# Freeing space for the down weights, x first and one weight order for all tiles in a fused attention + gated-layer kernel

## The chip, the cores and the metric

The kernel runs on one core of a Trainium2 chip. The metric is device time in microseconds (us); lower is better. Every run quoted is fast, that is, within 1.5% of the fastest run of the same kernel. PE is TensorE, ACT is ScalarE, DVE is VectorE, SP is the queue that issues most transfers.

## The reference, cut to what matters

```python
# S = 2048 tokens, D = 1024; H = 32 query heads of Dh = 32, ONE key/value head; F = 3584; bf16
def A(x):   # attention on the normalised x
    q = x @ wq; k = x @ wk; v = x @ wv
    p = softmax(einsum("bhqd,bkd->bhqk", q, k) * Dh**-0.5)
    return einsum("bhqk,bkd->bhqd", p, v) @ wo
def B(x):   # gated layer on the normalised h
    return (sigmoid(x @ w_gate) * (x @ w_up)) @ w_down
h  = x + A(layernorm(x))
h2 = h + B(layernorm(h))
```

There are 16 tiles of 128 tokens. A tile's scores go in 32 *visits*: one visit is 8 PE matmuls (scores) and two ACT exponentials of 128x1024. In all there are 512 visits and 1024 exponentials.

## The kernel before

The order of every instruction is fixed when the program is built. The kernel contains a small planner: it keeps a clock for each engine, adds an assumed cost for each instruction, and emits on PE whatever its clocks say is ready. Score matmuls have priority, so that ACT never runs dry; the gated layer (gate/up "GU", down "D") fills the rest, and when the planner thinks that nothing is ready it emits a *filler* matmul. The main loop, cut:

```python
while True:
    t = pl.free["pe"]
    ...
    if can_s and run - t < 750.0:      # ACT's queue is short: emit the scores of visit v
        emit_S(v); v += 1; emit_PV(t); continue
    ...                                # else go on with the current group, or pick one:
    # PRIO = ["xT", "KV", "Q0", "OP", "GU", "D", "Q"]
    ...
    if v and spare:                    # nothing is ready: filler
        pl.op("pe", mm(F_ps[:, spare[0], 0:256], ident[:, :], kT4[:, 0:256], True, True), ...)
```

One memory zone is used twice: first for the normalised, transposed x (four quarters), wq and the K/V weights, later for all 28 pieces of w_down:

```python
wq_sb = zview(DT * S, DT, D)
...
def free_wd(last):                      # called as projections finish
    for i in list(wd_left):             # 7 groups of 4 pieces
        if (i < 4 and q_left4[i] == 0 and 2 * i in k_ev and 2 * i + 1 in k_ev) or \
                (i >= 4 and q_left[0] == 0 and len(k_ev) == NT // 2):
            wd_left.remove(i); load_wd(4 * i, 4, [last])
```

Gate/up weights go through a ring of 22 pieces of 256 KB. A piece is kept while the planner sees a use ahead that is near. The order of uses was special for the first two tiles, so that they share pieces; D of any tile needs all of w_down:

```python
TP = [(0, p) for p in range(5)] + [(1, 4), (1, 3), (0, 5), (1, 5), (0, 6), (1, 6)] + [(1, p) for p in (2, 1, 0)]
TP += [(t, p) for t in range(2, NT) for p in (reversed(range(NFP)) if t % 2 else range(NFP))]
```

The softmax row sums of the first four groups (a group is eight of the 32 heads for one tile) were made on PE, by matmuls with a matrix of ones (cut). Later groups add on DVE and use four such matmuls. The start:

```python
load_x([0]); load_x([1])
wk_ld = dma(lambda: ACT.dma_start(wk_sb, ...), "wk", ..., ring="act")
wv_ld = dma(lambda: ACT.dma_start(wv_sb, ...), "wv", ..., ring="act")
load_wq(0, 2); load_x([2, 3]); load_wq(2, 4); load_x([4, 5])
...
if v == 0 and known([c_id, c_w], t):   # warm-up matmuls until the first transposes are ready
    pl.op("pe", mm(S_ps[:, 5, :], ident[:, :], hact[:, 0:512], True, True), [c_id, c_w], **t_mm(512))
```

The softmax here doesn't subtract the row's maximum and nothing guards it: scores larger than these inputs give would overflow.

Of the kernel before, what the change touches and what calls it, by code (L numbers as in the profile page):

```python
# [128 lines left out]
def bass_sequential_preLN__grouped_kv_mqa__glu_gated_glu__prompt_kernel(  # L129
# [21 lines left out]
    NI = 2 * NFP  # L151
    TP = [(0, p) for p in range(5)] + [(1, 4), (1, 3), (0, 5), (1, 5), (0, 6), (1, 6)] + [(1, p) for p in (2, 1, 0)]
    TP += [(t, p) for t in range(2, NT) for p in (reversed(range(NFP)) if t % 2 else range(NFP))]
    ITEMS = [(t, p, w) for t, p in TP for w in range(2)]
# [6 lines left out]
    NPS = 16  # L161
    NX = 4
    NB = 3
    NPC = 22
# [8 lines left out]
    with ExitStack() as es:  # L173
# [43 lines left out]
        def xnT(dt, a, n):  # L217
            return xnT4[a // 512][:, dt, a % 512:a % 512 + n]
        wq_sb = zview(DT * S, DT, D)
        o3 = DT * S + DT * D  # L220
# [73 lines left out]
        def load_wq(a, b, deps=()):  # L294
            o = dma(lambda: SP.dma_start(wq_sb[:, :, a * P:b * P], A_wq[:, a * P:b * P].rearrange("(a p) n -> p a n", p=P)),
                    f"wq{a}", D * P * (b - a) * 2, deps, prio=0)
            for g in range(a, b):
                wq_ld[g] = o

        load_x([0])  # L300
        load_x([1])
        wk_ld = dma(lambda: ACT.dma_start(wk_sb, A_wk.rearrange("(a p) j -> p a j", p=P)), "wk", P * DT * DH * 6, prio=0,
                    ring="act")
        wv_ld = dma(lambda: ACT.dma_start(wv_sb, A_wv.rearrange("(a p) j -> p a j", p=P)), "wv", P * DT * DH * 6, prio=0,
                    ring="act")
        load_wq(0, 2)
# [76 lines left out]
        def mm(o, l, r, start, stop, **kw):  # L383
            return lambda: PE.matmul(o, lhsT=l, rhs=r, start=start, stop=stop, **kw)  # L384

# [45 lines left out]
        q_left4 = [2 * NG, 2 * NG, NG, NG]  # L431
        wd_ld = []

        def mk_KV(p):
# [27 lines left out]
        def mk_Q(g, tok, n):  # L462
            def atoms(b):
                return [(mm(F_ps[:, b, 0:n], wq_sb[:, dt, g * P:(g + 1) * P], xnT(dt, tok, n),
                            dt == 0, dt == DT - 1), n, []) for dt in range(DT)]

            def after(b, last):
                q_left[0] -= 1
                q_left4[tok // 512] -= 1
                free_wd(last)  # L470
                early_loads(last)
                if tok == 0:
                    fa, fd = both(QTb[:, :, g, :], F_ps[:, b, 0:256].rearrange("p (a b) -> p a b", a=2))
                    ev = evac(fa, fd, 256, [last], 1)
                    q_ready[0][g] = q_ready[1][g] = ev
                else:
                    k = len(q_store)
                    s = k % NQS
                    deps = [last] + ([q_store[k - NQS]] if k >= NQS else [])
                    fa, fd = both(qst[:, s, 0:n], F_ps[:, b, 0:n])  # L480
                    ev = evac(fa, fd, n, deps, 1)
                    q_store.append(dma(lambda: SP.dma_start(q_dram[:, g, tok:tok + n], qst[:, s, 0:n]),
                                       f"qs{s}", P * 2 * n, [ev], prio=2))
                    for t in range(tok // P, (tok + n) // P):
                        q_of[t].append(q_store[-1])
                        load_q(t)
                return [ev]
            first = lambda: [wq_ld[g]] + [xT_ev[k] for k in range(tok // P, (tok + n) // P)]
            return Group("Q0" if tok == 0 else "Q", atoms, first, after)
# [20 lines left out]
        def free_wd(last):  # L510
            for i in list(wd_left):
                if (i < 4 and q_left4[i] == 0 and 2 * i in k_ev and 2 * i + 1 in k_ev) or \
                        (i >= 4 and q_left[0] == 0 and len(k_ev) == NT // 2):
                    wd_left.remove(i)
                    load_wd(4 * i, 4, [last])
# [39 lines left out]
        def reclaim(v):  # L555
            for sl, own in list(slot_owner.items()):
                if own in pv_done and (own[0] < NX or slot_add.get(sl) is not None):
                    slot_rel[sl] = [pv_done[own], slot_add.get(sl)]
                    del slot_owner[sl]
                    p_free.append(sl)  # L560
            if visits[v][0] >= NX:
                for sl in [sl for sl in p_free if sl >= NPS]:
                    p_free.remove(sl)

        def emit_S(v):
            G, kq = visits[v]
            qb, g = G // ND, 2 * (G % ND)
            deps = s_ready(v)
            pl.free["pe"] += 95.0
            last = None  # L570
            for kk in range(KB):
                for j in range(4):
# [5 lines left out]
                                 deps if (kk == 0 and j == 0) else [], occ=27.4, lat=27.4 + 150.0 + SEM)  # L578
            pl.free["pe"] += 111.0
            for i in range(2):  # L580
# [21 lines left out]
        sum_ev = {}  # L602
        sum_todo = collections.deque((G, kq) for G in range(NX, NT * ND) for kq in range(1, VPG))

        def flush_sums():
            while sum_todo:
                G, kq = sum_todo[0]
                if n_exp_of[G] <= kq or (kq == 1 and G > NX + 1 and (G - 2, 1) not in pv_done):
                    return
                sum_todo.popleft()  # L610
                for i in range(2):
                    T = Ts[:, G % 2, i * 1024:(i + 1) * 1024]
                    ins = [kq - 1, kq] if kq == 1 else [kq]
                    src = [pslot(slot_of[(G, q, i)]) for q in ins]
                    deps = [exp_of[(G, q, i)] for q in ins]
                    deps.append((pv_done.get((G - 2, 1)) if G > NX + 1 else None) if kq == 1 else sum_ev[(G, kq - 1, i)])
                    a, b = (src[0], src[1]) if kq == 1 else (T, src[0])
                    o = pl.op("dve", lambda T=T, a=a, b=b: DVE.tensor_tensor(out=T, in0=a, in1=b, op=ALU.add), deps,  # L618
                              prio=4, **t_dve(1024, 1.92))
                    for q in ins:  # L620
                        slot_add[slot_of[(G, q, i)]] = o
                    sum_ev[(G, kq, i)] = o
# [10 lines left out]
        def mk_PV(G, h):  # L633
            qb, g = G // ND, 2 * (G % ND)

            def block(b):
                r, rs = [], []
                k0, k1 = 8 * h, 8 * h + 8
                for kt in range(k0, k1):
                    kq, kk = kt // KB, kt % KB  # L640
                    for j in range(4):
# [3 lines left out]
                                    kt == k0, kt == k1 - 1, tile_position=(0, DH * j)))  # L645
                        if G < NX:
                            rs.append(mm(F_ps[DH * j:DH * (j + 1), b, 256:512], ones[:, :], pslot(slot)[:, co:co + 256],
                                         kt == k0, kt == k1 - 1, tile_position=(0, DH * j)))
                for j in range(4 if G >= NX and h else 0):
                    r.append(mm(F_ps[DH * j:DH * (j + 1), b, 256:512], ones[:, :],  # L650
                                Ts[:, G % 2, j * 512:j * 512 + 256], True, True, tile_position=(0, DH * j)))
# [46 lines left out]
            def first():  # L698
                r = [exp_of[(G, kq, i)] for kq in range(VPH * h, VPH * (h + 1)) for i in range(2)]
                r += [v_ev.get(p) for p in range(4 * h, 4 * h + 4)]  # L700
                return r + [c_v1] + ([merge_ev.get(G)] if G >= NX and h else [])

# [4 lines left out]
        def emit_PV(t):  # L707
# [8 lines left out]
            b = min(banks, key=lambda b: max([0.0] + [o.end for o in bank_rel[b]]))  # L716
            deps = gr.first() + list(bank_rel[b])
            for fn in gr.atoms(b):
                o = pl.op("pe", fn, deps, occ=27.4, lat=27.4 + 220.0 + SEM)
                o.tag = "PV"  # L720
                deps = []
            pl.free["pe"] += 109.0
            bank_rel[b] = gr.after(b, o)
# [42 lines left out]
        def flush_hT():  # L766
            while late_hT and (late_hT[0] < 2 or (late_hT[0] - 2) in gu_last):
# [4 lines left out]
                for i in range(len(ITEMS)):  # L772
                    if ITEMS[i][0] == t if t > 1 else (ITEMS[i][0] < 2 and t == 0):
                        queues["GU"].append(mk_GU(i))
# [146 lines left out]
        while True:  # L921
# [15 lines left out]
            if sd is None and queues["PV"]:  # L937
                pl.free["pe"] += 95.0
                if emit_PV(t):
                    idle = 0  # L940
                    continue
                pl.free["pe"] -= 95.0
            if cur is not None:
                fn, n, deps, *cb = cur[1][cur_i]
                if known(deps, t) or not can_s:
                    o = pl.op("pe", fn, deps + (cur[2] if cur_i == 0 else []), **t_mm(n))
                    o.tag = cur[0].cls
# [33 lines left out]
            if v == 0 and known([c_id, c_w], t):  # L981
                pl.op("pe", mm(S_ps[:, 5, :], ident[:, :], hact[:, 0:512], True, True), [c_id, c_w], **t_mm(512))
                continue
            idle += 1
            spare = [b for b in range(2) if known(bank_rel[b], t) and (cur is None or b != cur_b)]
            if v and spare:
                pl.op("pe", mm(F_ps[:, spare[0], 0:256], ident[:, :], kT4[:, 0:256], True, True), [k_ev[0]] + list(bank_rel[spare[0]]), **t_mm(256))
                continue
# [108 lines left out]
```

## Time and profile before

The time was 1109.71 us (1109.67 to 1110.74 in three runs).

| what | before |
|---|---|
| first exponential | 19.8 us |
| last projection matmul of Q ends, gated layer starts | 136 us |
| visit 480 of 512 starts | 964.8 us |
| last exponential ends | 1028 us |
| end of the profiled run | 1109.1 us |

Visits are found by counting blocks of eight score matmuls in the timeline of PE. Caution: in this trace 166 of the 12306 PE matmul records are missing (12140 matmuls stand beside 12306 weight loads), so PE's busy time is too small by a little; the transfers, ACT and the score matmuls are complete.

The table of stretches of before: start and end, length, then busy us (and instructions) of PE, weight loads, DVE, ACT and POOL, then PE's granted clock, share of DMA and GB/s. The first row is from the middle, the second from the tail.

```profile
400.00:440.00 40.00, 38.70 (x480) 16.93 (x486) 34.96 (x68) 39.98 (x45) 1.15 (x2) 1.00 0.75 185
...
1040.00:1080.00 40.00, 38.72 (x177) 17.51 (x180) 9.27 (x18) 4.18 (x7) 0.79 (x2) 1.00 1.10 267
```

In the middle ACT has no idle time and PE hardly any. In the tail ACT's exponentials are done and PE works off the gated layer. The same view for two stretches that the change touches:

```profile
58.00:92.00 34.00, 32.95 (x636) 21.92 (x634) 14.51 (x36) 33.24 (x37) 0.00 (x0) 1.00 0.81 247
150.00:180.00 30.00, 27.57 (x348) 12.85 (x350) 26.46 (x53) 29.26 (x33) 1.33 (x2) 1.00 1.00 252
```

The start, from the timeline of before (start, length, engine, line, operation, out<-in, count, and in brackets the idle time ahead of it with what ended it):

```profile
0.72 0.46 ACTq L302 DMA_DIRECT2D zone<-in_A_wk_dram  x1
...
1.67 10.94 PE L384 MATMUL S_ps<-hact,ident 128*128 128x512 bf16 x40 [1.67 <-POOL ident L278]
...
4.32 1.33 ACT L315 ACTIVATE zone<-zone 128x256 bf16<-128x256 bf16 x4 [0.98 <-DMA zone<-in_A_wk_dram]
...
8.57 0.88 DVE L371 TENSOR_SCALAR ring<-ring,rstd 128x1024 bf16<-128x1024 bf16 x2
...
12.44 1.06 PE L389 MATMUL F_ps<-ident,ring 128*128 128x128 bf16 x16
...
19.37 0.40 PE L384 MATMUL S_ps<-QTb,kT 32*128 32x256 bf16 x8
...
19.82 1.94 ACT L588 ACTIVATE Pr<-S_ps 128x1024 bf16<-128x1024 f32 x2 [0.73 <-PE S_ps L384]
```

x is normalised at 9.45 us (8.57 + 0.88), but its transposes stand behind 40 warm-up matmuls until 12.4. wk had arrived at 4.3.

What happens when Q is done, first on the SP queue, then on PE (two timelines of before):

```profile
144.29 2.94 SPq L493 DMA_DIRECT2D zone<-in_B_w_down_dram  x6
...
151.17 0.82 SPq L493 DMA_DIRECT2D zone<-in_B_w_down_dram  x2
152.04 2.74 SPq L817 DMA_DIRECT2D ring<-in_B_w_up_dram  x2
```

```profile
151.75 2.03 PE L384 MATMUL F_ps<-kT,ident 128*128 128x256 bf16 x17
...
157.74 0.39 PE L384 MATMUL F_ps<-ring,hnT 128*128 128x512 bf16 x1 [1.14 <-DMA ring<-in_B_w_up_dram]
```

The ring gets its first refill only after the last down weights. PE runs out of weights: 17 fillers in a row, then a wait.

The chain of waits, in its last stretch (start, length, what):

```profile
1030.35 4.84 DMA ring<-in_B_w_gate_dram
1035.24 9.89 PE F_ps L384 x45
...
1074.52 5.10 DMA ring<-in_B_w_gate_dram
1079.66 9.89 PE F_ps L384 x45
```

The end is PE's, with two waits for ring pieces in it.

### The profile page before, as it was taken

The numbers are of one execution on the slowest core, as the hardware profiler recorded it, in microseconds if no ns is written. First come the engines' busy times: TensorE is split into PE (matmuls) and PEld (weight loads), VectorE is DVE, ScalarE is ACT, GpSimd is POOL, SyncE is SP. The second block draws the span as 40 slices with busy tenths as digits, with TensorE's granted clock in tenths as the row PEclk, the third lists the DMA queues.
The fourth block names the chain that finished last, engine by engine and source line by source line (L and its number), as shares of the span: only waits on it lengthen the run. The fifth ranks groups of instructions, "written<-read, shape, count | busy, mean of one in ns | idle before, by whom it ended". The sixth has DMA issues, their size and how long they took to land.

```text
span 1109.1 us, 29973 instructions
## 1 busy us (share of the span) xinstructions
PE 1061.8 (96%) x12140; PEld 475.8 (43%) x12306; DVE 884.5 (80%) x1727; ACT 1011.6 (91%) x1162; POOL 27.9 (3%) x56
## 2 busy tenths in 40 slices
PE   9999989999999999999999999999999999999998
PEld 5664344343344444444444444444444444344443
DVE  7747988798888989798888989798888988788411
ACT  4999999999999999999999999999999999999110
POOL 1100000000000000000000000000000000000000
PEclk9999999999999999999999999999999999999999
DMA  9976399928769595968869595977869595976991
GB/s 231 202 236 199 99 255 282 275 53 232 206 144 251 144 253 131 262 189 196 238 149 247 142 257 130 259 194 188 242 149 243 149 251 138 253 190 180 260 264 43
DMA packets 304730, 222.06 MB, mean 200 GB/s; under 512 B 121552, under 2 KB 295888, under 8 KB 304592
## 3 DMA queue, kind: packets, MB, share of 16 engines
q1 hardware_dynamic: 302512, 220.01, 78.4%
q8 instruction: 97, 1.59, 0.6%
q10 hardware_dynamic: 2080, 0.13, 0.1%
q14 instruction: 41, 0.34, 0.1%
HBM read 189.66 MB, written 7.86 MB: 178 GB/s over the span
## 4 chain that ended last, share of the span: by engine, by line
PE 82%; ACT 8%; issue 4%; DVE 4%; DMA 2%; SPq 0%; POOL 0%; POOLq 0%
PE F_ps L384 68%; PE S_ps L384 14%; ACT Pr L588 8%; DMA ring<-in_B_w_gate_dram 1%; ACT tnh L860 1%; DVE Ts L618 1%; DMA ring<-in_B_w_up_dram 1%; DVE st L325 1%; DVE st L323 0%; DVE ring L371 0%; DVE ring L364 0%; DVE hact L274 0%; SPq L817 0%; DVE hst L864 0%; DVE mv L327 0%
## 5 line engine op out<-in xcount | busy, mean ns | idle before, releaser
L588 ACT ACTIVATE Pr<-S_ps 128x1024 bf16<-128x1024 f32 x1014 | 951.4, 1054 | 6.6 <-PE S_ps L384 5.6
L618 DVE TENSOR_TENSOR Ts<-Ts,Pr 128x1024 bf16<-128x1024 bf16 x720 | 475.3, 679 | 40.6 <-ACT Pr L588 36.9
L384 PE MATMUL F_ps<-ring,hnT 128*128 128x512 bf16 x1671 | 418.4, 381 | 19.3 <-issue 11.7
L384 PEld LDWEIGHTS F_ps<-ring,hnT 128*128 128x128 bf16 x1754 | 149.7, 98 | 223.0 <-issue 79.1
L384 PE MATMUL F_ps<-zone,hact 128*128 128x512 bf16 x839 | 210.2, 381 | 6.3 <-issue 6.0
L384 PE MATMUL S_ps<-QTb,kT 32*128 32x256 bf16 x4096 | 203.4, 273 | 8.9 <-ACT Pr L588 5.6
L384 PEld LDWEIGHTS S_ps<-QTb,kT 32*128 32x128 bf16 x4096 | 61.0, 92 | 192.1 <-ACT Pr L588 131.9
L384 PE MATMUL F_ps<-Pr,Vb 128*32 128x256 bf16 x4056 | 134.5, 274 | 0.1
L864 DVE SCALAR_TENSOR_TENSOR hst<-tnh,F_ps 128x512 bf16<-128x512 f32 x112 | 76.5, 683 | 62.9 <-PE F_ps L384 60.1
L384 PEld LDWEIGHTS F_ps<-zone,hact 128*128 128x128 bf16 x896 | 76.2, 98 | 103.7 <-issue 32.3
L860 ACT ACTIVATE tnh<-F_ps 128x512 f32<-128x512 f32 x112 | 71.3, 637 | 46.6 <-PE F_ps L384 46.6
L384 PEld LDWEIGHTS F_ps<-Pr,Vb 128*32 128x32 bf16 x4056 | 97.1, 96 | 36.4 <-DVE hst L864 10.9
L618 DVE TENSOR_TENSOR Ts<-Pr 128x1024 bf16<-128x1024 bf16 x120 | 80.5, 688 | 37.3 <-ACT Pr L588 37.1
L384 PE MATMUL F_ps<-zone 128*128 128x256 bf16 (+2 forms) x568 | 74.2, 274 | 5.1 <-DVE mvr L335 1.2
L384 PE MATMUL F_ps<-wo_sb,OT 128*128 128x512 bf16 x239 | 59.6, 380 | 2.5 <-issue 2.5
L384 PEld LDWEIGHTS F_ps<-zone 128*128 128x128 bf16 x576 | 42.6, 97 | 29.5 <-issue 8.8
L894 DVE SCALAR_TENSOR_TENSOR h_sb<-F_ps,h_sb 128x512 bf16<-128x512 f32 x32 | 21.9, 685 | 35.6 <-PE F_ps L384 35.6
L625 DVE TENSOR_TENSOR Ts<-Ts 128x1024 bf16<-128x1024 bf16 x60 | 41.4, 689 | 1.5
L337 POOL TENSOR_SCALAR zb<-mvb 128x1 bf16<-128x1 bf16 (+1 forms) x24 | 10.5, 437 | 1012.5 <-DVE mvb L333 1012.5
L384 PEld LDWEIGHTS F_ps<-wo_sb,OT 128*128 128x128 bf16 x256 | 22.4, 98 | 29.3 <-issue 6.7
L685 DVE STREAM_TRANSPOSE Rc<-Ri 128x256 f32<-128x256 f32 x64 | 28.1, 439 | 0.1
L668 DVE TENSOR_TENSOR Oc<-F_ps,Oc 128x256 f32<-128x256 f32 x60 | 25.2, 420 | 3.5 <-PE F_ps L384 2.1
(59 smaller groups left out, 349.0 us busy)
## 6 DMA issues: line engine op xcount, KB each, us to landing
ring<-in_B_w_gate_dram SPq DMA_DIRECT2D x308, 256.0 KB, 4.0
ring<-in_B_w_up_dram SPq DMA_DIRECT2D x307, 256.0 KB, 4.3
zone<-in_B_w_down_dram SPq DMA_DIRECT2D x28, 256.0 KB, 3.9
h_sb<-in_A_x_dram SPq DMA_DIRECT2D x16, 256.0 KB, 5.3
out_dram<-h_sb SPq DMA_DIRECT2D x32, 128.0 KB, 2.6
ring<-in_A_x_dram SPq DMA_DIRECT2D x7, 512.0 KB, 5.6
QTb<-q_scratch SPq DMA_DIRECT2D x14, 256.0 KB, 4.5
Pr<-in_B_w_up_dram SPq DMA_DIRECT2D x9, 256.0 KB, 4.0
```

Of the source, the lines that this page charges most:

```text
L325: b = pl.op("dve", lambda k=k, src=src: DVE.bn_stats(st[:, k, 1, :], src[:, 512:1024]), dep, prio=prio, occ=590, lat=756, order=[st_user.g ...
L337: f = pl.op("pool", lambda: POOL.tensor_scalar(out=zb[:, ph, sl].unsqueeze(2), in0=mvb[:, ph, sl, 1:2], scalar1=LN_EPS_BF16, scalar2=None, ...
L384: return lambda: PE.matmul(o, lhsT=l, rhs=r, start=start, stop=stop, **kw)
L588: exps[u] = pl.op("act", lambda slot=slot, pb=pb: ACT.activation(out=pslot(slot).rearrange("p (a b) -> p a b", a=2), in_=S_ps[:, pb:pb + 2 ...
L618: o = pl.op("dve", lambda T=T, a=a, b=b: DVE.tensor_tensor(out=T, in0=a, in1=b, op=ALU.add), deps, prio=4, **t_dve(1024, 1.92))
L625: merge_ev[G] = pl.op("dve", lambda T4=T4: DVE.tensor_tensor(out=T4[:, :, 0, :], in0=T4[:, :, 0, :], in1=T4[:, :, 1, :], op=ALU.add), [sum ...
L668: a = pl.op("dve", lambda: DVE.tensor_tensor(out=Oc[:, :], in0=O, in1=Ob, op=ALU.add), [last, oc_ev[G], o_ev.get(G - 1)], prio=0, **t_dve( ...
L685: d = pl.op("dve", lambda: DVE.transpose(out=Rc[:, :], in_=Ri[:, :].unsqueeze(2).to_broadcast([P, 2 * P // DH, DH])), [r], prio=2, **t_dve ...
L860: tanh_of[n] = pl.op("act", lambda: ACT.activation(out=tnh[:, n % 2, :], in_=F_ps[:, b, :], func=ACTF.Tanh, scale=0.5), [last, tn_user.get ...
L864: e = pl.op("dve", lambda: DVE.scalar_tensor_tensor(out=hst[:, n % NST, :], in0=tnh[:, n % 2, :], scalar=1.0, in1=F_ps[:, b, :], op0=ALU.a ...
L894: e = pl.op("dve", lambda: DVE.scalar_tensor_tensor(out=h_sb[:, t % 4, sl], in0=F_ps[:, b, :], scalar=0.5, in1=h_sb[:, t % 4, sl], op0=ALU ...
```

## The change

Its intent: let w_down load earlier (each half of wq and the K/V weights give up their space by themselves), give x tiles 0 and 1 the transfer engines alone, use one order of weights that turns round from tile to tile, so that tile 0 is finished and its D can run early. It also puts the second-half row sums of groups 0 to 3 on DVE, counts the warm-up matmuls of the first 5.2 us at 429 ns instead of 216 (the trace of before starts the first ones every 0.43 us, those after 5.9 us every 0.21), and makes the planner charge a mode switch of PE, a change between the forms `128*128`, `32*128` and `128*32` of the timelines, only where the mode changes (in the trace of before, from 161.98 us, seven `128*128` matmuls and the change to the next scores take 1.61 us, which is 7 x 0.216 and 0.10). The diff, cut to its core (`NCR = 0` switches off some new code, which is left out):

```diff
-    TP = [(0, p) for p in range(5)] + [(1, 4), (1, 3), (0, 5), (1, 5), (0, 6), (1, 6)] + [(1, p) for p in (2, 1, 0)]
-    TP += [(t, p) for t in range(2, NT) for p in (reversed(range(NFP)) if t % 2 else range(NFP))]
+    TP = [(t, p) for t in range(NT) for p in (reversed(range(NFP)) if t % 2 else range(NFP))]
@@
-        wq_sb = zview(DT * S, DT, D)
+        wq2 = [zview(DT * S + h * DT * 512, DT, 512) for h in range(2)]
@@
-        wk_ld = dma(lambda: ACT.dma_start(wk_sb, ...), "wk", P * DT * DH * 6, prio=0, ring="act")
+        wk_ld = dma(lambda: ACT.dma_start(wk_sb, ...), "wk", P * DT * DH * 6, [x_ld[1]], prio=0, ring="act")
         # ... wv the same
@@ free_wd
-                        (i >= 4 and q_left[0] == 0 and len(k_ev) == NT // 2):
+                        (i in (4, 5) and all(q_done[g] == S for g in range(4 * i - 16, 4 * i - 12))) or \
+                        (i == 6 and len(k_ev) == NT // 2):
@@ emit_S, emit_PV
-            pl.free["pe"] += 95.0
+            enter("row")      # adds 0.09 to 0.10 us, and only when the mode changes
@@ row sums
-                        if G < NX:
+                        if h == 0 and G < NX:
                             rs.append(mm(..., ones[:, :], pslot(slot)[:, co:co + 256], ...))
-                for j in range(4 if G >= NX and h else 0):
+                for j in range(4 if h else 0):
                     r.append(mm(..., ones[:, :], Ts[:, G % 2, j * 512:j * 512 + 256], True, True, ...))
@@ GU groups of a tile are queued when its hT is issued
-                    if ITEMS[i][0] == t if t > 1 else (ITEMS[i][0] < 2 and t == 0):
+                    if ITEMS[i][0] == t:
@@ warm-up
-                pl.op("pe", mm(S_ps[:, 5, :], ...), [c_id, c_w], **t_mm(512))
+                pl.op("pe", mm(S_ps[:, 5, :], ...), [c_id, c_w], **t_mm(512 if t > 5200.0 else 1024))
```

More of the change, by code (lines that the diff above doesn't have):

```diff
@@ L162, in bass_sequential_preLN__grouped_kv_mqa__glu_gated_glu__prompt_kernel @@
     NX = 4
+    NCR = 0
     NB = 3
@@ L294, in load_wq @@
         def load_wq(a, b, deps=()):
-            o = dma(lambda: SP.dma_start(wq_sb[:, :, a * P:b * P], A_wq[:, a * P:b * P].rearrange("(a p) n -> p a n", p=P)),
+            o = dma(lambda: SP.dma_start(wq2[a // 4][:, :, a % 4 * P:(a % 4 + b - a) * P], A_wq[:, a * P:b * P].rearrange("(a p) n -> p a n", p=P)),
                     f"wq{a}", D * P * (b - a) * 2, deps, prio=0)
@@ L301, in bass_sequential_preLN__grouped_kv_mqa__glu_gated_glu__prompt_kernel @@
         load_x([1])
-        wk_ld = dma(lambda: ACT.dma_start(wk_sb, A_wk.rearrange("(a p) j -> p a j", p=P)), "wk", P * DT * DH * 6, prio=0,
-                    ring="act")
-        wv_ld = dma(lambda: ACT.dma_start(wv_sb, A_wv.rearrange("(a p) j -> p a j", p=P)), "wv", P * DT * DH * 6, prio=0,
-                    ring="act")
+        wk_ld = dma(lambda: ACT.dma_start(wk_sb, A_wk.rearrange("(a p) j -> p a j", p=P)), "wk", P * DT * DH * 6, [x_ld[1]], prio=0, ring="act")
+        wv_ld = dma(lambda: ACT.dma_start(wv_sb, A_wv.rearrange("(a p) j -> p a j", p=P)), "wv", P * DT * DH * 6, [x_ld[1]], prio=0, ring="act")
         load_wq(0, 2)
@@ L383, in mm, with enter, emit_mm @@
         def mm(o, l, r, start, stop, **kw):
-            return lambda: PE.matmul(o, lhsT=l, rhs=r, start=start, stop=stop, **kw)
+            fn = lambda: PE.matmul(o, lhsT=l, rhs=r, start=start, stop=stop, **kw)
+            if not kw:
+                fn.col = lambda: [mm(o[DH * j:DH * (j + 1)], l[:, DH * j:DH * (j + 1)], r, start, stop,
+                                     tile_position=(0, DH * j)) for j in range(4)]
+            return fn
+        mode = ["full"]
+        col_run = [0]
+        DRAIN = {"full": 96.0, "row": 92.0, "col": 100.0}
+        def enter(m):
+            if mode[0] != m:
+                pl.free["pe"] += DRAIN[mode[0]]
+                mode[0] = m
+                col_run[0] = 0
+        def emit_mm(fn, n, deps):
+            if mode[0] == "col" and hasattr(fn, "col") and col_run[0] < NCR:
+                col_run[0] += 1
+                for f in fn.col():
+                    o = pl.op("pe", f, deps, occ=n / 9.6 + 1.2, lat=n / 9.6 + 171.0 + SEM)
+                    deps = []
+                return o
+            enter("full")
+            return pl.op("pe", fn, deps, **t_mm(n))
         def mk_xT(t):
@@ L432, in bass_sequential_preLN__grouped_kv_mqa__glu_gated_glu__prompt_kernel @@
         wd_ld = []
+        q_done = collections.Counter()
         def mk_KV(p):
@@ L463, in atoms @@
             def atoms(b):
-                return [(mm(F_ps[:, b, 0:n], wq_sb[:, dt, g * P:(g + 1) * P], xnT(dt, tok, n),
+                return [(mm(F_ps[:, b, 0:n], wq2[g // 4][:, dt, g % 4 * P:(g % 4 + 1) * P], xnT(dt, tok, n),
                             dt == 0, dt == DT - 1), n, []) for dt in range(DT)]
@@ L469, in after @@
                 q_left4[tok // 512] -= 1
+                q_done[g] += n
                 free_wd(last)
@@ L556, in reclaim @@
             for sl, own in list(slot_owner.items()):
-                if own in pv_done and (own[0] < NX or slot_add.get(sl) is not None):
+                if own in pv_done and ((own[0] < NX and own[1] == 0) or slot_add.get(sl) is not None):
                     slot_rel[sl] = [pv_done[own], slot_add.get(sl)]
@@ L578, in emit_S @@
                                  deps if (kk == 0 and j == 0) else [], occ=27.4, lat=27.4 + 150.0 + SEM)
-            pl.free["pe"] += 111.0
+            pl.free["pe"] += 18.0
             for i in range(2):
@@ L602, in bass_sequential_preLN__grouped_kv_mqa__glu_gated_glu__prompt_kernel, with k_first @@
         sum_ev = {}
-        sum_todo = collections.deque((G, kq) for G in range(NX, NT * ND) for kq in range(1, VPG))
+        def k_first(G):
+            return VPH if G < NX else 0
+        sum_todo = collections.deque((G, kq) for G in range(NT * ND) for kq in range(k_first(G) + 1, VPG))
         def flush_sums():
@@ L607, in flush_sums @@
                 G, kq = sum_todo[0]
-                if n_exp_of[G] <= kq or (kq == 1 and G > NX + 1 and (G - 2, 1) not in pv_done):
+                k1 = k_first(G) + 1
+                if n_exp_of[G] <= kq or (kq == k1 and G > 1 and (G - 2, 1) not in pv_done):
                     return
@@ L612, in flush_sums @@
                     T = Ts[:, G % 2, i * 1024:(i + 1) * 1024]
-                    ins = [kq - 1, kq] if kq == 1 else [kq]
+                    ins = [kq - 1, kq] if kq == k1 else [kq]
                     src = [pslot(slot_of[(G, q, i)]) for q in ins]
                     deps = [exp_of[(G, q, i)] for q in ins]
-                    deps.append((pv_done.get((G - 2, 1)) if G > NX + 1 else None) if kq == 1 else sum_ev[(G, kq - 1, i)])
-                    a, b = (src[0], src[1]) if kq == 1 else (T, src[0])
+                    deps.append(pv_done.get((G - 2, 1)) if kq == k1 else sum_ev[(G, kq - 1, i)])
+                    a, b = (src[0], src[1]) if kq == k1 else (T, src[0])
                     o = pl.op("dve", lambda T=T, a=a, b=b: DVE.tensor_tensor(out=T, in0=a, in1=b, op=ALU.add), deps,
@@ L700, in first @@
                 r += [v_ev.get(p) for p in range(4 * h, 4 * h + 4)]
-                return r + [c_v1] + ([merge_ev.get(G)] if G >= NX and h else [])
+                return r + [c_v1] + ([merge_ev.get(G)] if h else [])
             gr = Group("PV", block, first, after)
@@ L717, in emit_PV @@
             deps = gr.first() + list(bank_rel[b])
+            enter("col")
+            col_run[0] = 0
             for fn in gr.atoms(b):
@@ L721, in emit_PV @@
                 deps = []
-            pl.free["pe"] += 109.0
+            pl.free["pe"] += 9.0
             bank_rel[b] = gr.after(b, o)
@@ L937, in bass_sequential_preLN__grouped_kv_mqa__glu_gated_glu__prompt_kernel @@
             if sd is None and queues["PV"]:
-                pl.free["pe"] += 95.0
                 if emit_PV(t):
@@ L941, in bass_sequential_preLN__grouped_kv_mqa__glu_gated_glu__prompt_kernel @@
                     continue
-                pl.free["pe"] -= 95.0
             if cur is not None:
@@ L945, in bass_sequential_preLN__grouped_kv_mqa__glu_gated_glu__prompt_kernel @@
                 if known(deps, t) or not can_s:
-                    o = pl.op("pe", fn, deps + (cur[2] if cur_i == 0 else []), **t_mm(n))
+                    o = emit_mm(fn, n, deps + (cur[2] if cur_i == 0 else []))
                     o.tag = cur[0].cls
@@ L981, in bass_sequential_preLN__grouped_kv_mqa__glu_gated_glu__prompt_kernel @@
             if v == 0 and known([c_id, c_w], t):
-                pl.op("pe", mm(S_ps[:, 5, :], ident[:, :], hact[:, 0:512], True, True), [c_id, c_w], **t_mm(512))
+                pl.op("pe", mm(S_ps[:, 5, :], ident[:, :], hact[:, 0:512], True, True), [c_id, c_w],
+                      **t_mm(512 if t > 5200.0 else 1024))
                 continue
@@ L986, in bass_sequential_preLN__grouped_kv_mqa__glu_gated_glu__prompt_kernel @@
             if v and spare:
+                enter("full")
                 pl.op("pe", mm(F_ps[:, spare[0], 0:256], ident[:, :], kT4[:, 0:256], True, True), [k_ev[0]] + list(bank_rel[spare[0]]), **t_mm(256))
```

## The prediction

> **What bounds the kernel now.** Two engines are nearly full. The table of stretches shows ScalarE (ACT) busy 39.98 of every 40 us from 400 to 960 us (the groups: 1014 exponentials, 951 us), TensorE (PE) 38.8 of 40. The last exponential ends near 1027 us, but the run lasts to 1109: in its last 75 us PE is busy 69.5, working off about two token tiles of the gated layer (168 matmuls x 0.216 us = 36 us each); the chain of waits ends in PE. That backlog was built early, since the gated layer starts only at 136 us. So the end is set by PE's sum: work, idle and filler. PE time saved early should come off the tail nearly one for one.
>
> **Losses that the change touches.**
> 1. Start. DVE has normalised x tiles 0 and 1 at 9.45 us, but the timeline shows 40 warm-up matmuls ahead of the transposes until 12.2 us: the first ones start every 0.43 us, later ones every 0.21; the planner counted 0.216 for all. [...] Counting 429 until 5.2 us drops about 10 of them: transposes near 10.2, first exponential near 18 instead of 19.8. Loading x first is worth a few tenths: tile 1's statistics follow tile 0's without a wait. Gain 2 us (estimate).
> 2. Row sums by ones-matmuls: 256 in groups 0 to 3. The second halves go to DVE: 112 fewer matmuls at 0.03 us = 3.5 us of PE. DVE gains 24 adds and 4 merges of 0.69 us = 19 us, mainly at 58 to 92 us, where it is 45% busy; it nearly fills.
> 3. Down weights. Twelve pieces (3 MB) wait for the last projection, are issued from 136.2 to 151.8 us, and the ring's first refills come behind them, at 152. PE runs 21 fillers at 150 to 154, waits 1.1 us at 157, then 6 fillers and small waits by 178: about 5 us in all. After: one third is free when K and V are done, one third four groups earlier, four loads remain at the end.
> 4. Order. Tiles 0 and 1 share fewer pieces: about 10 more loads of 256 KB (estimate; 10 us at the 275 GB/s of 160 to 200 us). But tile 0 finishes after seven pairs, and its 12 us of down products can fill DMA waits. Gain of 3 and 4 together: 4 us.
>
> The planner's new accounting of mode switches differs only for neighbouring stages; +-1 us.
>
> **Sum.** 2 + 3.5 + 4 = 9.5, less 1 for crowding on DVE: 1109.7 - 8.5 = about **1101 us**, 8 in 10 between **1094 and 1107**. Faster by over 2% 0.03, within 0.95, slower 0.02.
>
> **What would show each step.** First exponential at 17.5 to 18.5 us, 30 to 40 warm-up matmuls in all. Ones-matmuls on probabilities 256 to 128; DVE over 80% in 58 to 92. At most 6 down loads issued after the last projection; fillers after 140 us from 27 to under 10. Gate/up loads about 10 above 632. Middle unchanged; exponentials ending 2 to 4 us sooner; the stretch after them about 75 us instead of 82.
>
> **What would make it wrong.** The x loads or the DVE chain pace the first 45 us, so the earlier start is given back; tile 0, unshared, starves on the ring for longer; DVE, full from 58 to 136 us, holds PSUM banks; down weights at 40 to 120 us crowd the Q round trip. A gain over 15 us needs idle in the middle to shrink.

The 2 us rest on the starts in the trace, 0.43 and 0.21 us apart, and the sum is 9.5 less 1.

## The result, and the profile after

The changed kernel took 1105.57 us (1102.97 to 1107.11, four runs) against 1109.69 of before in the same rounds: ratio 0.996, 95% interval 0.9938 to 0.9983. A second set (the control below) gave 0.9944 (0.9932 to 0.9956). A ratio is the mean time of a kernel's fast runs over the mean of the fast runs of before in the same rounds, so it is not quite the ratio of the medians quoted.

| what | before | after |
|---|---|---|
| first exponential | 19.8 us | 21.2 us |
| warm-up matmuls (by their weight loads) | 50 | 38 |
| Q ends | 136.2 us | 134.8 us |
| down-weight loads issued after that | 16 | 8 |
| fillers, all / after 140 us | 32 / 27 | 8 / 4 |
| gate/up loads | 633 | 656 |
| visit 480 | 964.8 us | 968.2 us |
| matmuls of the output projection and gated layer left at visit 480 | 524 | 499 |
| from visit 480 to the end | 144.3 us | 134.5 us |
| end of the profiled run | 1109.1 us | 1102.7 us |

The time did not come off evenly. At visit 480 the changed kernel is 3.4 us *behind*; it then ends 9.8 us sooner from there. Of these, 25 fewer matmuls at 0.216 us (nine take 2.12 us, of which 0.39 is the last one's own length) are 5.4 us, and ring waits of PE after 955 us (3.0 us before, 0.3 after) are 2.7 us. The list of waits of before also has 0.9 us for ACT there, that of after none; 0.8 us are not attributed.

The middle and the tail in the table of stretches of after. PE's fuller column is not a finding: this trace misses no matmul record.

```profile
400.00:440.00 40.00, 40.00 (x456) 16.48 (x455) 35.38 (x69) 40.00 (x46) 0.79 (x2) 1.00 0.63 166
...
1040.00:1080.00 40.00, 40.00 (x187) 18.15 (x186) 9.94 (x18) 4.18 (x7) 0.79 (x2) 1.00 1.04 282
```

```profile
58.00:92.00 34.00, 34.00 (x512) 20.54 (x513) 28.18 (x59) 33.50 (x37) 0.00 (x0) 1.00 0.95 295
150.00:180.00 30.00, 26.95 (x318) 11.45 (x320) 24.01 (x49) 27.57 (x33) 1.60 (x2) 0.94 0.85 239
```

DVE went from 43% to 83% busy in 58 to 92 us, as forecast. But look at 150 to 180: ACT was idle for 2.4 us there, against 0.7 before, and the granted clock fell to 0.94.

The start of after (timeline):

```profile
1.67 7.98 PE L382 MATMUL S_ps<-hact,ident 128*128 128x512 bf16 x28 [1.67 <-POOL ident L278]
...
4.30 0.43 ACTq L302 DMA_DIRECT2D zone<-in_A_wk_dram  x1
...
4.77 0.64 ACTq L303 DMA_DIRECT2D zone<-in_A_wv_dram  x1
...
9.54 1.07 PE L411 MATMUL F_ps<-ident,ring 128*128 128x128 bf16 x16
...
13.81 1.33 ACT L313 ACTIVATE zone<-zone 128x256 bf16<-128x256 bf16 x4 [1.67 <-DMA zone<-in_A_wk_dram]
...
17.67 2.93 PE L382 MATMUL F_ps<-zone 128*128 128x256 bf16 x31 [3.16 <-DMA zone<-in_A_wv_dram]
...
20.53 0.61 PE L382 MATMUL S_ps<-QTb,kT 32*128 32x256 bf16 x8
...
21.20 1.02 ACT L613 ACTIVATE Pr<-S_ps 128x1024 bf16<-128x1024 f32 x1 [1.42 <-PE S_ps L382]
```

The transposes do start 2.9 us sooner. Then the head start is lost: wk comes at 13.8, and PE waits 3.16 us for wv, until 17.7. In this trace the clock was also halved from 18.9 to 22.3 us; in the control (a_again) it was not, and the first exponential came at 20.8. The transfer lists show the late landing; the last column is the time from issue to landing in us. First before, then after:

```profile
zone<-in_A_wk_dram ACTq DMA_DIRECT2D x1, 64.0 KB, 3.6
zone<-in_A_wv_dram ACTq DMA_DIRECT2D x1, 64.0 KB, 4.9
```

```profile
zone<-in_A_wk_dram ACTq DMA_DIRECT2D x1, 64.0 KB, 9.5
zone<-in_A_wv_dram ACTq DMA_DIRECT2D x1, 64.0 KB, 12.8
```

They now run beside the 256 to 1024 KB loads of wq and x: issued at 0.7 and 1.2 us in before, at 4.3 and 4.8 in after, with five of SP's loads already issued. These two have ACT's queue to themselves, and yet took 9.5 and 12.8 us while SP's loads were in flight. They are also made of tiny rows: the profile's queue list has 2080 packets and 0.13 MB for ACT's queue (q10), about 63 bytes each. No run separates the tiny rows from the late issue.

When Q is done, SP and PE of after (two timelines):

```profile
136.20 4.47 SPq L517 DMA_DIRECT2D zone<-in_B_w_down_dram  x6
141.16 1.20 SPq L899 DMA_TRANSPOSE hact<-hst  x1
142.47 1.05 SPq L848 DMA_DIRECT2D ring<-in_B_w_up_dram  x2
...
152.38 1.22 SPq L899 DMA_TRANSPOSE hact<-hst  x1
153.65 1.08 SPq L848 DMA_DIRECT2D ring<-in_B_w_up_dram  x2
```

```profile
158.28 0.39 PE L382 MATMUL F_ps<-ring,hnT 128*128 128x512 bf16 x1 [2.97 <-DMA ring<-in_B_w_up_dram]
158.61 0.40 PE L382 MATMUL S_ps<-QTb,kT 32*128 32x256 bf16 x8
158.93 1.90 PE L382 MATMUL F_ps<-Pr,Vb 128*32 128x256 bf16 x32
...
165.42 1.06 PE L382 MATMUL F_ps<-Pr,Vb 128*32 128x256 bf16 x32
```

The refills start 10 us sooner (142.5 for 152.0) and the fillers are gone, but one wait of 2.97 us is left, and the 32 matmuls just after it take 1.90 us where the same group takes 1.06 us later. The records of the clock show half (0.50) from 158.9 to 162.3 us. Before had no such loss: its wait there was 1.14 us, behind 17 fillers, and its clock stayed at 1.00. In other traces the same wait was 2.56 us (a_again), 2.86 (n_ring2) and 3.36 (e_hoist), each with a half clock just after it (32 matmuls in 1.90 us in a_again and n_ring2; a mean clock of 0.94 from 150 to 180 us in n_ring2 and e_hoist); in n_swap it was 1.11 us, and the clock stayed at 1.00. What decides whether the clock falls is not shown.

The tail of after, in the chain of waits, is one piece of PE work to the end:

```profile
1028.72 71.04 PE F_ps L382 x359
```

### The profile page after: what moved, and what is told of

Its sections match the earlier page's. It is cut to its first block, busy times and chain, and to the rows that moved or that the text cites. A ratio compares the mean times of both kernels' runs of the same rounds, so it can differ in the third digit from the quotient of the medians.

```text
span 1102.7 us, 29947 instructions
## 1 busy us (share of the span) xinstructions
PE 1083.4 (98%) x12158; PEld 471.3 (43%) x12158; DVE 903.5 (82%) x1753; ACT 1010.1 (92%) x1164; POOL 23.2 (2%) x56
## 3 DMA queue, kind: packets, MB, share of 16 engines
q10 hardware_dynamic: 2080, 0.13, 0.1%
## 4 chain that ended last, share of the span: by engine, by line
PE 85%; ACT 6%; DMA 4%; DVE 3%; issue 2%; ACTq 0%; SPq 0%; DVEq 0%
PE F_ps L382 72%; PE S_ps L382 13%; ACT Pr L613 5%; DMA ring<-in_B_w_gate_dram 2%; DVE Ts L647 1%; DMA zone<-in_A_wv_dram 1%; DMA ring<-in_B_w_up_dram 1%; ACT tnh L891 0%; DVE hact L274 0%; DMA zone<-ring 0%; DMA ring<-in_A_x_dram 0%; DVE Oc L697 0%; DVE Rc L709 0%; DVE h_sb L777 0%; DVE Ts L654 0%
## 5 line engine op out<-in xcount | busy, mean ns | idle before, releaser
L647 DVE TENSOR_TENSOR Ts<-Ts,Pr 128x1024 bf16<-128x1024 bf16 x732 | 483.9, 680 | 48.9 <-ACT Pr L613 45.7
L382 PE MATMUL F_ps<-ring,hnT 128*128 128x512 bf16 x1760 | 441.2, 381 | 6.3 <-DMA ring<-in_B_w_up_dram 4.0
L382 PE MATMUL F_ps<-zone,hact 128*128 128x512 bf16 x896 | 224.7, 381 | 0.0
L647 DVE TENSOR_TENSOR Ts<-Pr 128x1024 bf16<-128x1024 bf16 x126 | 85.9, 683 | 55.6 <-ACT Pr L613 55.6
L891 ACT ACTIVATE tnh<-F_ps 128x512 f32<-128x512 f32 x112 | 73.8, 659 | 50.4 <-PE F_ps L382 50.4
L382 PE MATMUL F_ps<-zone 128*128 128x256 bf16 (+2 forms) x576 | 76.7, 279 | 6.3 <-DMA zone<-in_A_wv_dram 3.2
L382 PE MATMUL F_ps<-wo_sb,OT 128*128 128x512 bf16 x256 | 64.3, 381 | 0.1
L654 DVE TENSOR_TENSOR Ts<-Ts 128x1024 bf16<-128x1024 bf16 x64 | 43.9, 685 | 0.6
L335 POOL TENSOR_SCALAR zb<-mvb 128x1 bf16<-128x1 bf16 (+1 forms) x24 | 6.1, 253 | 1018.0 <-DVE mvb L331 1018.0
```

The costliest lines, as they stand in the source:

```text
L335: f = pl.op("pool", lambda: POOL.tensor_scalar(out=zb[:, ph, sl].unsqueeze(2), in0=mvb[:, ph, sl, 1:2], scalar1=LN_EPS_BF16, scalar2=None, ...
L382: fn = lambda: PE.matmul(o, lhsT=l, rhs=r, start=start, stop=stop, **kw)
L647: o = pl.op("dve", lambda T=T, a=a, b=b: DVE.tensor_tensor(out=T, in0=a, in1=b, op=ALU.add), deps, prio=4, **t_dve(1024, 1.92))
L654: merge_ev[G] = pl.op("dve", lambda T4=T4: DVE.tensor_tensor(out=T4[:, :, 0, :], in0=T4[:, :, 0, :], in1=T4[:, :, 1, :], op=ALU.add), [sum ...
L891: tanh_of[n] = pl.op("act", lambda: ACT.activation(out=tnh[:, n % 2, :], in_=F_ps[:, b, :], func=ACTF.Tanh, scale=0.5), [last, tn_user.get ...
```

## The experiments

Two questions: did PE's sum of work, filler and waits set the time, as predicted, and what became of each part? Theory S (sum): every microsecond of PE saved early shows at the end. Rival A: ACT paces the middle and PE has slack. Rival P (pattern): the planned order settles into one of a few repeating patterns, so a part's worth depends on what else is in.

Names beginning with a are the changed kernel with one part undone; with b, the kernel before with one part added. All these are re-planned. Names with e or n keep the changed kernel's planned order on PE (n_run1100 excepted). All gave correct results but e_light, which is wrong.

**a_again.** No edit.

> The changed kernel unaltered, as control on the same chip. Expected 0.996 of before (1105.5 us), first exponential at 21.2 us, wait of the K/V projection for wv about 3 us, ring wait about 3 us near 155 us.

Measured: 1103.36 us, before 1110.3, ratio 0.9944 (0.9932 to 0.9956). First exponential 20.8 us, ring wait 2.56 us. The profiled run ended at 1101.3. This is the control for the others.

**a_kv.** wk and wv issued at the start again.

```diff
-        wk_ld = dma(..., [x_ld[1]], prio=0, ring="act")     # wv the same
+        wk_ld = dma(..., prio=0, ring="act")
```

> The changed kernel, but wk and wv issued at the start as before, not after x tile 1. Theory T1 (the late wk/wv is a loss that reaches the end): wk and wv land by about 6 us, first exponential at 17.5 to 18.5 us instead of 21.2, no 3 us wait for wv, total 3 us below the changed kernel (about 1102.5). Rival T2 (the start is absorbed later, by the ring wait at 155 us or by the x chain): first exponential earlier just the same, total within 1 us of the changed kernel.

Measured: 1102.69 us, ratio 0.994 (0.9928 to 0.9951). The first exponential came at 17.9 us and visit 480 at 958.7, 8.1 us ahead of the control. Yet the end was the same, for the re-planned order had 524 matmuls left there and needed 141.9 us instead of 134.5. By the total T2 holds, but not for the reason that it gives: nothing was absorbed by a wait; another order was run. So this run does not say what the late wk/wv cost. e_hoist below does.

**a_order.** The old order of tiles 0 and 1.

```diff
+    TP = [(0, p) for p in range(5)] + [(1, 4), (1, 3), (0, 5), (1, 5), (0, 6), (1, 6)] + [(1, p) for p in (2, 1, 0)]
+    TP += [(t, p) for t in range(2, NT) for p in ...]       # and the queueing of tile 1 with tile 0
```

> The changed kernel with the old interleaved order of tiles 0 and 1. T1 (the unshared order starves the ring): gate/up loads back from 656 to about 632, the 3 us ring wait and the slow clock at 155 to 162 us gone, total 2 to 4 us below the changed kernel. Rival T2 (the straight order is worth it since tile 0's down products come early): total 2 us or more above the changed kernel.

Measured: 1110.03 us, ratio 1.0004 (0.9991 to 1.0017): the rival. 52 fillers instead of 8 (44 at 0.11 us, as 17 take 2.03 us with the last one's 0.27, are 4.8 us), 524 matmuls left at visit 480, and 2.5 us of ring waits after 955 us. I had feared the straight order; here it is worth about 6.7 us (0.0060 of 1110). T1 falls in its mechanism too: with the old order PE still waits 2.40 us for the ring at 155.9, with the half clock after it.

**a_ones.** Row sums of the second halves back on PE.

```diff
-                        if h == 0 and G < NX:
+                        if G < NX:
-                for j in range(4 if h else 0):
+                for j in range(4 if G >= NX and h else 0):
```

> The changed kernel with the second-half row sums of groups 0 to 3 again by 128 ones-matmuls on PE instead of DVE adds. T1 (PE time counts one for one): total 3 to 4 us above the changed kernel. Rival T2 (the fuller DVE at 58 to 92 us gave it back): within 1 us of the changed kernel.

Measured: 1112.55 us, ratio 1.0027 (1.0014 to 1.004), 9.2 us above the control (0.0083 of 1110). The 112 matmuls are only 2.8 us (32 of them take 1.06 us, less 0.27 for the last one's latency, so 0.025 us each). The profiled runs reach visit 480 at the same time (967.0 and 966.9); the whole difference lies after it, 142.8 against 134.5 us, with 524 matmuls left against 499. Neither theory had this size.

**e_hoist.** Order frozen; only wk and wv go first and wait for nothing.

```diff
+        for o in (wv_ld, wk_ld):          # after planning
+            o.deps = []
+            lists["act"].remove(o); lists["act"].insert(0, o)
```

> The changed kernel with the order of every engine frozen; only the two issues of wk and wv are moved to the head of ACT's queue and no longer wait for x tile 1. Theory L (late wk/wv costs time that reaches the end when nothing is replanned): first exponential near 18 us instead of 20.8 to 21.2, all milestones about 3 us earlier, total about 3 us below the changed kernel of 1103.4, near 1100.5. Rival (the head start is taken back by the ring wait at 155 us or later): total within 1 us of 1103.4.

Measured: 1102.23 us, ratio 0.9933 (0.9919 to 0.9946); the interval overlaps the control's. In the traces the gain is plain and shrinks on its way: against a_again 3.5 us at visit 0, 2.7 at visit 64, 2.2 at visit 80 (the ring wait grew from 2.56 to about 3.4 us), 1.7 at the end. The K/V wait is gone (timeline of e_hoist):

```profile
14.74 2.20 PE L382 MATMUL F_ps<-zone 128*128 128x256 bf16 x31
...
16.88 0.40 PE L382 MATMUL S_ps<-QTb,kT 32*128 32x256 bf16 x8
...
17.33 1.02 ACT L613 ACTIVATE Pr<-S_ps 128x1024 bf16<-128x1024 f32 x1 [0.48 <-PE S_ps L382]
```

So the late wk/wv cost 3.5 us at the start. About half of that reached the end by these two traces; but two traces of one program, after and a_again, ended 1.4 us apart, so the size at the end is not firm.

**e_light.** Less ACT work in ten tiles, order frozen.

```diff
+ n = 448 if 128 <= v < 448 else 512
- in_=S_ps[:, pb:pb + 2, :]
+ in_=S_ps[:, pb:pb + 2, 0:n]
```

> Wrong result on purpose: the changed kernel, same order, but the exponentials of visits 128 to 447 (10 tiles) take 896 of 1024 columns, which takes about 0.1 us off each on ACT, 6 to 7 us per tile. Theory S (PE's sum sets the middle, as the prediction had it): the period of 62.3 us per tile stays within 0.2 us, total within 2 us of 1103.4. Rival A (ACT paces the middle and PE has hidden slack): the period falls by 0.5 to 1.5 us per tile to PE's own, total 5 to 15 us lower.

Measured (three rounds): 1102.55 us, ratio 0.9942 (0.9927 to 0.9956). The 0.1 us off an exponential was the estimate; one took 0.91 us on average from 300 to 800 us, 1.07 after 960. ACT was busy 625.4 us instead of 659.3 in 340 to 1000 us, but visits 128 to 448 took 62.22 us per tile instead of 62.43 in the control. Theory S: PE sets the middle of this order. The rows of the table of stretches, first of a_again, then of e_light:

```profile
340.00:1000.00 660.00, 659.61 (x7546) 273.32 (x7547) 571.80 (x1081) 659.31 (x750) 8.65 (x22) 1.00 0.76 198
...
340.00:1000.00 660.00, 659.62 (x7560) 275.32 (x7559) 573.34 (x1084) 625.44 (x752) 8.61 (x22) 1.00 0.76 199
```

**b_sum.** Before plus the row sums alone (the reverse of a_ones).

> The kernel before plus only the row sums of the second halves of groups 0 to 3 on DVE. Theory S (PE time saved counts one for one): 3 to 4 us below before, 1106.5. Rival P (the planned order falls back into the same repeating pattern, with 128.6 us of PE stream left at visit 480 of 512 as in before, so the 3.1 us saved are lost by there): within 1.5 us of before.

Measured: 1111.64 us, ratio 1.0025 (1.0011 to 1.0038): slower by 2.8 us (0.0025 of 1110). Neither expectation holds in size: S said 3 to 4 us faster, P within 1.5 us. The backlog of 524 is the one that P named. With the fillers counted the direction fits a sum on PE: 37 more of them (69 against 32) are 4.1 us, more than the 2.8 saved; that makes 1.3 of the 2.8 us lost. Saved PE time is only worth something if useful work is ready to take its place, and here much of it went to fillers.

**b_wd_order.** Before plus the space for w_down and the straight order.

> The kernel before plus only the down-weight space and the straight order, the two terms that the prediction put at 4 us together. The order settles at 128.6 us left at visit 480 as before does, with 30 fillers against 32. If the prediction's size holds on its own: ratio 0.996 to 0.997. Rival (the gain needs the whole change, since only it settles at 123.2 us left): ratio 0.999 to 1.001.

Measured: 1109.52 us, ratio 0.9992 (0.998 to 1.0004). 30 fillers, 524 matmuls left at visit 480, as in before. The two parts alone gain nothing that can be told from zero.

**a_wd.** The changed kernel with w_down loaded as before.

```diff
-                        (i in (4, 5) and all(q_done[g] == S for ...)) or (i == 6 and len(k_ev) == NT // 2):
+                        (i >= 4 and q_left[0] == 0 and len(k_ev) == NT // 2):   # and one wq buffer
```

> The changed kernel with the down weights loaded as before (twelve pieces only after the last projection), straight order kept. Theory (space and order need each other): 43 fillers instead of 8 and 133.7 us of PE stream left at visit 480 instead of 123.2, ring waits of several us at 150 to 200; total 7 to 14 us above the changed kernel, ratio 1.001 to 1.007. Rival (the terms are independent, space alone is worth about 3 us): ratio 0.996 to 0.998.

Measured: 1117.88 us, ratio 1.0061 (1.0043 to 1.008), 13 us above the control (0.0117 of 1110): 43 fillers, 548 matmuls left at visit 480. Straight order without the space is harmful, space without the straight order is worth nothing (a_order). Of the orders tried, only the whole change gives 8 fillers. No run undoes the planner's new accounting of mode switches or of the slow first warm-up matmuls, which re-plan as well, so their share is not known.

**n_run1100.** An attempt to have both the early start and the short backlog, by re-planning a_kv with another threshold.

```diff
-                if can_s and run - t < 750.0:
+                if can_s and run - t < 1100.0:
```

> The changed kernel with wk/wv issued at the start and the planner's threshold for issuing scores raised from 750 to 1100 ns of queued ACT work. Rival P (what counts is the pattern that the order settles into: here a short backlog as in the changed kernel, plus an early start): attention about as early as in a_kv or 3 us later, stretch after visit 480 near 133 us instead of 142, total 1093 to 1098. Theory S: PE's useful stream is the same 937 us as in the changed kernel, so total within 2 us of a_kv, 1101 to 1104.

Measured: 1108.42 us, ratio 0.9991 (0.9979 to 1.0004). The backlog at visit 480 was short (498 matmuls), but visit 480 came late (968.7 us), after 32 fillers and 4.2 us of waits for gate pieces between 340 and 1000 us. Neither expectation: a short backlog late is not enough.

**n_ring2.** e_hoist, and the last down-weight loads take turns with the first ring refills; PE's order is unchanged, instruction for instruction.

```diff
-                fn, key, nbytes, deps, sink = paced.popleft()
+                k = next((j for j, it in enumerate(paced) if it[1][:2] == "sl"), 0) if v > 48 else 0
+                turn[0] += 1
+                if turn[0] % 2 == 0: k = 0
+                fn, key, nbytes, deps, sink = paced[k]; del paced[k]
```

> The changed kernel with wk/wv hoisted as in e_hoist, and with the last down-weight loads taking turns with the first ring refills instead of going ahead of them; the order on PE is unchanged, instruction for instruction. Theory R (the ring wait of 3 us near 155 us and the slow clock after it come from the refills standing behind the last down-weight loads): first refill issued about 4 us sooner, wait under 1 us, clock in 150 to 180 back to 1.00, total 3 to 5 us below e_hoist (ratio 0.9933), near 0.990. Rival (the straight order simply needs more ring bandwidth than there is in that stretch): the wait only moves, ratio within 0.0015 of e_hoist.

Measured: 1100.72 us, ratio 0.991 (0.9897 to 0.9923). The first refill went out at 133.6 us instead of 138.7 (e_hoist), but the wait stayed at 2.86 us (3.36 in e_hoist) and the clock at 0.94. Theory R falls, though the ratio lies 0.0023 under that of e_hoist, outside what the rival allowed; the traces end 0.6 us apart and the intervals overlap. In the SP timeline the piece that was missed had been issued just behind a transposition of gated products, which itself waited for DVE (transpositions on SP waited 5.2 us for DVE in 136 to 158 us, 2.5 us the longest); the loads behind it went out only after it, at 149.67 us (timelines of n_ring2, SP, then PE):

```profile
148.41 1.22 SPq L906 DMA_TRANSPOSE hact<-hst  x1
149.67 1.08 SPq L855 DMA_DIRECT2D ring<-in_B_w_up_dram  x2
...
154.20 0.50 PE L389 MATMUL F_ps<-ring,hnT 128*128 128x512 bf16 x1 [2.86 <-DMA ring<-in_B_w_up_dram]
```

**n_swap.** n_ring2, and in six places that transposition lets up to two ring loads pass.

```diff
+        for o in [o for o in sp if o.key and o.key[:2] == "ha"][:6]:
+            i = sp.index(o)
+            for _ in range(2):
+                if sp[i + 1].key[:2] == "sl":
+                    sp[i], sp[i + 1] = sp[i + 1], sp[i]; i += 1
```

> n_ring2 with the order of all engines but SP's unchanged; on SP's in-order queue the first six transpositions of the gated products, where ring loads stand just behind them, let up to two of those go ahead. Theory Q (the 3 us ring wait comes from the two up pieces standing behind a transposition that itself waits for VectorE): these two pieces are issued 2 to 3 us sooner, the wait near 154 us falls from 2.9 to under 1 us, the clock in 150 to 180 is back to 1.00, total 3 to 5 us below n_ring2, ratio 0.987 to 0.989. Rival (the two pieces wait anyway, for the pacing that ties them to an exponential, or for bandwidth): wait stays over 2 us, ratio 0.990 to 0.992.

Measured: 1099.31 us, ratio 0.9903 (0.9887 to 0.992). SP and PE of n_swap (two timelines), then its table of stretches:

```profile
148.93 0.90 SPq L855 DMA_DIRECT2D ring<-in_B_w_up_dram  x2
149.87 1.23 SPq L906 DMA_TRANSPOSE hact<-hst  x1
```

```profile
152.59 0.39 PE L389 MATMUL F_ps<-ring,hnT 128*128 128x512 bf16 x1 [1.11 <-DMA ring<-in_B_w_up_dram]
...
157.02 0.59 PE L389 MATMUL F_ps<-ring,hnT 128*128 128x512 bf16 x2 [1.14 <-DVE Ri L719]
```

```profile
150.00:180.00 30.00, 25.41 (x318) 10.83 (x320) 25.81 (x51) 28.55 (x33) 1.60 (x2) 1.00 1.08 264
```

The wait fell from 2.86 to 1.11 us and the clock stayed at 1.00 (this trace misses 184 PE records, so its PE column is low). A new wait of 1.14 us, for DVE, came at 157.0: by the idle time only 0.6 us were saved, and the rest of the gain fits the half clock that did not come. Visit 72 came 1.8 us sooner than in n_ring2 and the profiled run ended 2.4 us sooner (1096.6). So it is shown in the trace that the transposition held the loads back; the size is below the 3 to 5 us expected, and the ratio alone cannot tell it from n_ring2. Against the changed kernel's control (0.9944) n_swap is lower with intervals that do not meet: it beats both kernels, by less than 2%.

The runs in one table. Times are of the profiled runs; "left" counts the matmuls of output projection and gated layer behind visit 480 in the program.

| run | ratio | fillers | left | visit 480 | then to the end |
|---|---|---|---|---|---|
| before | 1 | 32 | 524 | 964.8 | 144.3 |
| b_sum | 1.0025 | 69 | 524 | 967.2 | 142.0 |
| b_wd_order | 0.9992 | 30 | 524 | 965.1 | 143.6 |
| a_again | 0.9944 | 8 | 499 | 966.9 | 134.5 |
| a_kv | 0.994 | 22 | 524 | 958.7 | 141.9 |
| a_order | 1.0004 | 52 | 524 | 964.1 | 145.7 |
| a_ones | 1.0027 | 22 | 524 | 967.0 | 142.8 |
| a_wd | 1.0061 | 43 | 548 | 970.0 | 146.5 |
| n_run1100 | 0.9991 | 32 | 498 | 968.7 | 136.2 |
| e_light | 0.9942 | 8 | 499 | 966.7 | 134.5 |
| e_hoist | 0.9933 | 8 | 499 | 965.1 | 134.5 |
| n_ring2 | 0.991 | 8 | 499 | 964.5 | 134.5 |
| n_swap | 0.9903 | 8 | 499 | 962.1 | 134.5 |

With the order frozen (the four rows with 8 fillers that end the table, and a_again), the last stretch is the same to 0.1 us, and what is still ahead at visit 480 reaches the end. Where the program is re-planned, "left" jumps between a few values and moves the end by more than the part that was edited.

The backlog is not a cause of its own, though. In the traces without missing matmul records, PE's time can be added up without a remainder: matmuls from start to start, fillers, and the idle time ahead of each. Against a_again, the 8.5 us that the trace of a_ones is longer are 2.9 of ones-matmuls, 1.7 of fillers and 3.7 of idle time; the 8.5 us of a_order are 5.3 of fillers and 0.6 of idle time, and a second half-clock stretch of 3.41 us at 969.8; the 15.2 us of a_wd are 4.1 of fillers and 7.9 of idle time, and it has two half-clock stretches before 60 us. So the sum on PE that the prediction names holds for the re-planned orders too; what it could not say is how many fillers and waits the planner would put in.

## Why the prediction was right or wrong

The total was right: 1101 was forecast with 1094 to 1107, and 1105.57 was measured. The gain was 4.4 us by the first ratio and 6.2 by the second, for 8.5 forecast. The terms were not as good as the sum: the start missed by 3.2 us in the wrong direction, and the stretch after the last exponential, 71 us where about 75 was forecast, made up for it. That the total still fell in the range is in part luck.

- "So the end is set by PE's sum: work, idle and filler." Right, as far as tested: e_light shows it for the changed kernel's order, not for before. Shortening ACT's exponentials in ten tiles (e_light; 0.91 us on average from 300 to 800 us, 1.07 after 960) moved the period by 0.21 us per tile, and fillers explain about half of what b_sum lost.
- "PE time saved early should come off the tail nearly one for one." With the order frozen the traces bear it out in part (n_swap was 1.8 us ahead of n_ring2 at visit 72 and 2.4 at the end; e_hoist kept 1.7 of its 3.5 us). Wrong as a rule for this kernel, since an edit re-plans: the 2.8 us of ones-matmuls were worth 9.2 us in one order (a_ones, where 14 more fillers and 3.7 us of idle time came along) and minus 2.8 us in another (b_sum: 0.0025 of 1110).
- The start, "Gain 2 us (estimate)". This is the step that failed. The warm-up matmuls went from 50 to 38 and the transposes started 2.9 us sooner, as forecast. But I costed the move of wk and wv behind x at nothing. They landed 9.5 and 12.8 us after issue instead of 3.6 and 4.9, and the first exponential came at 21.2 us instead of 18. e_hoist took this back: 3.5 us at the first visit, 1.7 at the end.
- Row sums, "3.5 us of PE": measured 2.8 for the matmuls. DVE filled as forecast (83%).
- Down weights and order, "Gain of 3 and 4 together: 4 us". The fillers after 140 us fell from 27 to 4, as forecast (under 10). I counted twelve loads behind the last projection; there were 16, because the last quarter of x also frees four then, and 8 stayed (at most 6 forecast). The gate/up loads rose by 23, not about 10 (by 16 in b_wd_order, where only space and order changed). The size cannot be given as one number: together they gain nothing that shows on before (b_wd_order) and much in the changed kernel, where losing the order costs 6.7 us and losing the space 13 us.
- The ring was named under what would make the forecast wrong ("tile 0, unshared, starves on the ring for longer"). One wait at 155 us came, 2.97 us with a slow clock after it, but not for that reason: a_order shares the pieces and waits 2.40 us, and a_kv does not share them and has no wait over 0.5 us from 140 to 200 us. n_swap shows what a part of it was, an order on SP's queue that I had not read.
- "exponentials ending 2 to 4 us sooner; the stretch after them about 75 us instead of 82": the last exponential ends about 3 us *later* (1031.4 against 1028.3), and the stretch after it is 71 us. The gain sits in the tail.

Open: why the planner's order settles at 499, 524 or 548 matmuls left. I know the counts from the programs, not the rule. Also 0.8 us of the 9.8 gained after visit 480 are not attributed.

## What to carry to other kernels

When a kernel is list-scheduled at build time, undoing one part also changes the rest, so freeze the order and edit the lists after planning to measure one cost; and compare fillers and backlog at fixed points of the work before crediting a part. A small load that the first matmuls need belongs ahead of the large ones, not behind them: here it delayed the first x statistics by 0.3 us (3.87 against 3.60 us) and, put behind, came 6 to 8 us later after issue. When a load goes out late, see what the instruction just ahead of it on its queue was waiting for: here, letting two ring loads past a transposition shortened PE's wait from 2.86 us (n_ring2) to 1.11 (n_swap).
